# Attention and FFN on one core: a half's h and output tiles in pairs per PSUM bank, fewer scale operations, stores on SP's queue

## The chip, the core and the metric

The kernel runs on one core of a Trainium2 chip. Its engines are named as in the profile: PE (TensorE, matmuls; PEld its weight loads), DVE (VectorE), ACT (ScalarE), POOL (GpSimd) and SP (SyncE, which here only issues transfers). Each executes its own list of instructions in the order in which the program was built; semaphores tie the lists together. ACT and SP also issue DMAs, and such an issue stands in the engine's list like any other instruction. The metric is the device time of a run in microseconds (us), the median of several runs.

## The reference

```python
scores = scale * q @ k.T                                  # B=8, H=8, S=576, D=64
cum    = cumsum(maximum(s, 0))
scores = where(causal, -1e9, scores + minimum(-(cum_i - cum_j), 0))
attn   = softmax(scores) @ v
x      = attn.transpose(0, 2, 1, 3).reshape(4608, 512)
h      = x @ w_in                                         # 512 -> 2048
g      = where(h >= 1, h, where(h <= -1, 0, (h + 1)**2 / 4))
out    = g @ w_out                                        # 2048 -> 512
```

All inputs are fp32. The kernel computes each of the large products from f16 parts: every operand is scaled by powers of two and split into a high and a low half, and a product is three f16 matmuls (high x high, high x low, low x high).

## The kernel before

The work goes by batches of 576 tokens. A batch's tokens are the columns of its tiles, and they are cut into two halves (`HALF`): the first (`hf` 0) has 320 columns, the second (`hf` 1) 256.

**Attention** of a half is four jobs, one for each pair of heads. For a job, SP loads Q, K and V (`rq`, `rk` L337, `v` L254); ACT and DVE prepare them (L352 to L357); PE computes score tiles `s` (L412, L413); DVE masks them and takes the maximum `mn` (L418); ACT takes the exponential (L429, L451); POOL and DVE normalise and split (`rs` L445 and L446, `pb` L450 to L456); SP issues the DMA transposes `pt<-pb` (L457) and, once for both halves, `vt<-vb` (L383); PE multiplies them into `px` (L475); ACT and DVE write the half's f16 tile `x` (L486, L487). Score tiles and `px` share two PSUM banks.

**The FFN** of a half has 16 h tiles of 128 rows each. For tile `ft`, `ffn_h` lets PE put 12 matmuls into one of two PSUM banks `h` (L530). Then come, on 320 or 256 columns:

- ACT: `u` = Relu(us x h + ub) (L542);
- DVE: two passes, `h` = max(ws x h, u) (L545) and `u` = min(u, r) x h (L546);
- ACT: the f16 cast of `u`, g's high part (L556). `g_split` issues it behind the next tile's Relu, so that ACT's list runs Relu, cast of the tile before, Relu, cast;
- POOL: g's low part, `u` less the cast (L557).

`ffn_y` then lets PE put 12 matmuls into the four banks `y0` to `y3`, one for each 128 rows of the output (L569). The y matmuls of a tile follow its h by `Y_LAG` = 2 tiles, and run on into the h tiles of the next half. After the sixteenth, four evictions `o` scale the banks into SBUF (ACT, L583; at the very end DVE takes two, L581), and each is stored with a DMA of its own (L584), on ACT's queue but for two at the end.

The scales us, ws, ub, r and the output's ys are small tiles of a batch, made by `batch_scales` (13 DVE operations, behind the reduction that makes `a_in` once, L615) and `batch_y` (two per batch, L304). The first batch's are made at the end of the start-up, ahead of the loads of w_out, whose staging tiles are first written from `a_in` (L184, in `load`).

Attention of the halves to come is woven into the FFN of the half at hand: `attention_ffn` walks over FFN steps (one h tile or one y tile each) and inserts a slot of an attention job at set places. A scheduler then fixes each engine's list, by priorities (`FFN_LEAD` for the FFN's passes and evictions, `X_LEAD` for `x`) and by the buffers' dependences; `tc.issue_after` pins an instruction behind another. A wait of one instruction thus holds up everything behind it in its engine's list, SP's transposes behind SP's loads among them.

w_in is decoded and split ahead of the first FFN tile, w_out beside the first halves.

Of the kernel before, what the change touches and what calls it, by code (L numbers as in the profile page):

```python
# [71 lines left out]
def attention_ffn(ctx: ExitStack, tc: tile.TileContext, qT, kT, vT, s, w_in, w_out, yT):  # L72
# [201 lines left out]

    def batch_scales(b):
        m = msc[b]
        h = hsc[b] = ap.tile([P, 4], F32, tag="hs", name=f"hs{b}")
        V.tensor_scalar(h, w1.bound, m, 2.0 ** -27, ALU.mult, ALU.mult)
# [4 lines left out]
        V.tensor_scalar(r, r, 1.0, None, ALU.max)
# [1 line left out]
        V.tensor_scalar(r, r, 2.0 ** 14, None, ALU.mult)
        V.tensor_scalar(i, i, 23, None, ALU.logical_shift_right)
        V.tensor_scalar(i, i, 127, None, ALU.add)
        V.tensor_scalar(i, i, 1, 23, ALU.logical_shift_right, ALU.logical_shift_left)
# [4 lines left out]
        V.tensor_scalar(w, u, 2.0, None, ALU.mult)
# [227 lines left out]
    ffn_q, g4 = [], [None]  # L521

    def ffn_h(b, hf, ft):
        h_off, N, _ = HALF[hf]
        x = X[b, hf]
        h = ps_h.tile([P, 512], F32, tag="h", name=f"h{b}_{hf}_{ft}")
        n = 0
        for kt in range(NKT):
            for wl, xl in ((0, 0), (0, 1), (1, 0)):
                T.matmul(  # L530
                    h[:, :N], WI[4 * kt + ft // 4][:, wl, ft % 4 * P:(ft % 4 + 1) * P], x[:, kt, xl],
                    start=(n == 0), stop=(n == 3 * NKT - 1),
                )
# [4 lines left out]
        g = g4[0][:, ft % 4]
        with tc.high_priority(offset=FFN_LEAD):

            u = gp.tile([P, N], F32, tag="u", bufs=4, name=f"u{b}_{hf}_{ft}")
            first = A.activation(u, h[:, :N], AF.Relu, bias=ubi[b], scale=usc[b][:, fg:fg + 1]).ins  # L542
# [2 lines left out]
            V.scalar_tensor_tensor(h[:, :N], h[:, :N], wsc[b][:, fg:fg + 1], u, ALU.mult, ALU.max)  # L545
            V.scalar_tensor_tensor(u, u, r, h[:, :N], ALU.min, ALU.mult)  # L546
# [5 lines left out]
    def g_split(first=None):  # L552
        while to_split:
            g, u = to_split.pop()
            with tc.issue_after(first) if first is not None else ExitStack():
                A.copy(g[:, 0], u)  # L556
            G.tensor_tensor(g[:, 1], u, g[:, 0], ALU.subtract)  # L557

    ys = {}

    def ffn_y(b, hf, ft, g, ms=tuple(range(NKT))):
# [4 lines left out]
        for m in ms:
            c0 = ft % 2 * 2 * P + m % 2 * P
            for n, (wl, gl) in enumerate(((0, 0), (1, 0), (0, 1))):
                T.matmul(  # L569
                    ys[b, hf, m][:, :N], WO[8 * (m // 2) + ft // 2][:, wl, c0:c0 + P], g[:, gl],  # L570
                    start=(ft == 0 and n == 0), stop=(ft == NFT - 1 and n == 2),
                )
        if ft == NFT - 1:
            last = (b, hf) == (B - 1, len(HALF) - 1)
            for m in ms:
                tag, bufs = ("u", 4) if last and m >= 2 else ("o", O_BUFS)
                o = gp.tile([P, N], F32, tag=tag, bufs=bufs, name=f"o{b}_{hf}_{m}")
                y = ys[b, hf, m][:, :N]
                with tc.high_priority(offset=FFN_LEAD):
                    if last and m % 2:  # L580
                        V.tensor_scalar(o, y, ysc[b][m // 2], None, ALU.mult)  # L581
                    else:
                        A.activation(o, y, AF.Copy, scale=ysc[b][m // 2])  # L583
                (nc.sync if last and m % 2 else nc.scalar).dma_start(  # L584
                    yT[m * P:(m + 1) * P, b * S + h_off:b * S + h_off + N], o
                )
# [28 lines left out]
    V.tensor_reduce(a_in, w1.bound, axis=AX, op=ALU.max)  # L615
# [77 lines left out]
```

## Time and profile before

| | us |
|---|---|
| runs | 1110.91, 1114.15, 1114.35 |
| median | 1114.15 |
| the profiled execution's own time | 1111.73 |
| its span in the profile | 1109.9 |
| mean granted TensorE clock | 0.963 |
| PE busy | 1010.8 |
| DVE, ACT, POOL busy | 846.3, 725.8, 679.0 |

The profile is of one execution, which took 1111.73 us by the same clock as the runs; 1.8 us of that lie outside the span. Times in the trace count from the start of the span. In the first 145 us the weights are loaded and split, and PE is busy for 82.5 of them; from 275 us on, one batch after another takes 122 to 124 us; after 1013 us no attention is left, and only the FFN of the last batch runs. A row of waits gives the engine and line that waited, who released it, the total in us, how often, and the longest. A row of a group gives line, engine, operation, out<-in, the shape and the count, then busy us and mean ns of one, then the idle time ahead of it and what ended it. A row of the timeline gives start and duration in us, and in brackets the wait ahead of it.

### The profile page before, as it was taken

The numbers are of one execution on the slowest core, as the hardware profiler recorded it, in microseconds if no ns is written. First come the engines' busy times: TensorE is split into PE (matmuls) and PEld (weight loads), VectorE is DVE, ScalarE is ACT, GpSimd is POOL, SyncE is SP. The second block draws the span as 40 slices with busy tenths as digits, with TensorE's granted clock in tenths as the row PEclk, the third lists the DMA queues.
The fourth block names the chain that finished last, engine by engine and source line by source line (L and its number), as shares of the span: only waits on it lengthen the run. The fifth ranks groups of instructions, "written<-read, shape, count | busy, mean of one in ns | idle before, by whom it ended". The sixth has DMA issues, their size and how long they took to land.

```text
span 1109.9 us, 25082 instructions
## 1 busy us (share of the span) xinstructions
PE 1010.8 (91%) x8495; PEld 774.9 (70%) x8496; DVE 846.3 (76%) x2325; ACT 725.8 (65%) x1703; POOL 679.0 (61%) x1173
## 2 busy tenths in 40 slices
PE   2456898799999999999999999899999999899998
PEld 1232466587768877777778877687778877787787
DVE  7887966688787877787778877787777887887533
ACT  4765985677567774867567765777576765777432
POOL 4782795775556764766467664666476665765522
PEclk9955999799999999999999999999999999999999
DMA  7876653786468663886468763877387763676300
GB/s 235 218 200 192 170 87 91 158 173 155 100 122 188 148 152 71 187 162 158 79 146 177 161 136 81 177 160 163 68 176 155 165 137 74 158 156 138 68 25 19
DMA packets 340775, 155.01 MB, mean 140 GB/s; under 512 B 290856, under 2 KB 322472, under 8 KB 340648
## 3 DMA queue, kind: packets, MB, share of 16 engines
q1 hardware_dynamic: 330944, 143.49, 59.6%
q10 hardware_dynamic: 9704, 9.93, 2.9%
q8 instruction: 67, 1.10, 0.4%
q14 instruction: 60, 0.49, 0.1%
HBM read 72.31 MB, written 9.73 MB: 74 GB/s over the span
## 4 chain that ended last, share of the span: by engine, by line
PE 61%; DVE 12%; POOL 8%; DMA 7%; issue 6%; ACT 5%; ACTq 0%; SPq 0%; DVEq 0%; POOLq 0%
PE y L569 25%; PE h L530 25%; PE px L475 4%; DMA pt<-pb 3%; PE s L412 3%; PE s L413 3%; DVE pb L456 2%; ACT u L542 2%; POOL pb L453 2%; POOL pb L450 2%; DVE p L418 1%; DVE Q L357 1%; DMA vt<-vb 1%; POOL vb L371 1%; DVE h L545 1%
## 5 line engine op out<-in xcount | busy, mean ns | idle before, releaser
L530 PE MATMUL h<-x,WI 128*128 128x256 f16 (+1 forms) x3072 | 463.9, 290 | 7.4 <-ACT x L486 3.4
L569 PE MATMUL y<-g,WO 128*128 128x256 f16 (+1 forms) x3072 | 457.8, 288 | 7.0 <-POOL g L557 5.3
L530 PEld LDWEIGHTS <-WI 128*128 128x128 f16 x3072 | 291.1, 99 | 97.0 <-issue 13.9
L569 PEld LDWEIGHTS <-WO 128*128 128x128 f16 x3072 | 288.1, 98 | 92.9 <-issue 13.8
L557 POOL TENSOR_TENSOR g<-u,g 128x320 f16<-128x320 f32 (+1 forms) x256 | 206.0, 805 | 152.1 <-ACT g L556 151.6
L429 ACT ACTIVATE p<-p,mn 64x64 f32<-64x64 f32 (+4 forms) x320 | 179.4, 561 | 142.7 <-DVE mn L418 122.2
L542 ACT ACTIVATE u<-h,ub,us 128x320 f32<-128x320 f32 (+1 forms) x256 | 149.1, 583 | 120.3 <-PE h L530 115.3
L545 DVE SCALAR_TENSOR_TENSOR h<-h,ws,u 128x320 f32<-128x320 f32 (+1 forms) x256 | 132.4, 517 | 110.6 <-ACT u L542 108.1
L450 POOL TENSOR_SCALAR pb<-p,rs 64x128 f16<-64x128 f32 (+4 forms) x160 | 95.3, 596 | 171.2 <-DVE rs L446 112.1
L453 POOL TENSOR_TENSOR pb<-p,pb 64x128 f16<-64x128 f32 (+4 forms) x160 | 173.9, 1087 | 9.5
L456 DVE SCALAR_TENSOR_TENSOR pb<-p,rs,pb 64x128 f16<-64x128 f32 (+4 forms) x160 | 134.6, 841 | 47.1 <-POOL pb L450 47.0
L418 DVE CUSTOM_DVE_ANT_0 p<-s,mask 64x64 f32<-64x64 f32 (+4 forms) x320 | 134.4, 420 | 31.3 <-PE s L413 23.0
L412 PE MATMUL s<-K,Q 128*64 128x64 f32 (+1 forms) x336 | 126.2, 377 | 16.0 <-DVE mn L418 10.9
L546 DVE SCALAR_TENSOR_TENSOR u<-u,r,h 128x320 f32<-128x320 f32 (+1 forms) x256 | 130.3, 509 | 6.8 <-DVE h L545 0.5
L451 ACT ACTIVATE p<-p,rs 64x64 f32<-64x64 f32 (+4 forms) x160 | 89.6, 560 | 51.3 <-DVE rs L446 49.4
L556 ACT CAST g<-u 128x320 f16<-128x320 f32 (+1 forms) x256 | 107.9, 421 | 10.3 <-DVE u L546 10.3
L413 PE MATMUL s<-K,Q 68*64 68x64 f32 (+1 forms) x336 | 102.8, 307 | 2.1 <-DMA K<-cumd 1.3
L452 POOL TENSOR_SCALAR pb<-p 64x128 f16<-64x128 f32 (+4 forms) x160 | 93.2, 583 | 11.9 <-ACT p L451 11.0
L475 PEld LDWEIGHTS <-vt 128*64 128x64 f16 x1536 | 73.4, 113 | 36.7 <-issue 30.2
L475 PE MATMUL px<-pt,vt 128*64 128x256 f16 (+3 forms) x1536 | 83.5, 259 | 13.3 <-DMA pt<-pb 8.7
L412 PEld LDWEIGHTS s<-K,Q 128*64 128x64 f32 (+1 forms) x336 | 61.5, 183 | 27.3 <-DVE mn L418 8.2
L413 PEld LDWEIGHTS s<-K,Q 68*64 68x64 f32 (+1 forms) x336 | 61.9, 184 | 5.8 <-issue 1.7
(105 smaller groups left out, 983.0 us busy)
## 6 DMA issues: line engine op xcount, KB each, us to landing
...
```

The costliest lines, as they stand in the source:

```text
L412: T.matmul(sc[:R, :c1 - c0], Q1[:, hd, qo:qo + R], K1[:, hd, c0:c1], start=True, stop=False)
L413: T.matmul(sc[:R, :c1 - c0], Q2[:KC, hd, qo:qo + R], K2[:KC, hd, c0:c1], start=False, stop=True)
L418: ttr[0] = V.tensor_tensor_reduce(out=Pt[:R, c0:c1], in0=sc[:R, :c1 - c0], in1=mask[:R, mo:mo + c1 - c0], scale=-0.125 if j < F32_JOBS els ...
L429: A.activation(Pt[:R, :W], Pt[:R, :W], AF.Exp, bias=m2[:R], scale=-1.0, accum_out=sums[n, i][:R, hd:hd + 1])
L453: G.tensor_tensor(los[1], pw, his[1], ALU.subtract)
L456: V.scalar_tensor_tensor(los[0], pv, rs[:R, :1], his[0], ALU.mult, ALU.subtract)
L475: T.matmul(px[hd * D:(hd + 1) * D, lo:N], VT[:, vl * NB + j, hd * D:(hd + 1) * D], PT[:, 4 * j + 2 * hd + pl, lo:], start=(m == 0), stop=( ...
L530: T.matmul(h[:, :N], WI[4 * kt + ft // 4][:, wl, ft % 4 * P:(ft % 4 + 1) * P], x[:, kt, xl], start=(n == 0), stop=(n == 3 * NKT - 1),)
L542: first = A.activation(u, h[:, :N], AF.Relu, bias=ubi[b], scale=usc[b][:, fg:fg + 1]).ins
L545: V.scalar_tensor_tensor(h[:, :N], h[:, :N], wsc[b][:, fg:fg + 1], u, ALU.mult, ALU.max)
L557: G.tensor_tensor(g[:, 1], u, g[:, 0], ALU.subtract)
L569: T.matmul(ys[b, hf, m][:, :N], WO[8 * (m // 2) + ft // 2][:, wl, c0:c0 + P], g[:, gl], start=(ft == 0 and n == 0), stop=(ft == NFT - 1 an ...
```

## The change

Four things, of which the first is the largest.

1. In the second half (256 columns), two h tiles share a PSUM bank of 512 columns. Relu, both DVE passes, the cast and the low part then run once for a pair, on 512 columns. The four output tiles lie in pairs in the banks `y0` and `y1`; there are two evictions of 512 columns, in buffers of the `u` ring, and two stores of 128x2x256. Only the first tile of a y bank opens its accumulation with the start flag, and `issue_after` keeps the other's first matmul behind it.
2. `Y_LAG` is (2, 4): in the second half y follows h by four tiles, and up to two y tiles are issued in a step.
3. Of a batch's 13 + 2 scale operations 6 + 1 are left; factors that don't depend on the batch (`wb1`, `wb2`, 4 x `a_in`) are made once, `wb1` ahead of the first batch's scales.
4. All stores but the very last half's first are issued on SP's queue.

The first half's tiles and passes keep their shapes, and PE's list has the same number of instructions, 16170, in another order.

```diff
-Y_LAG = 2
+Y_LAG = (2, 4)
...
+    def weight_scales():
+        V.tensor_reduce(a_in, w1.bound, axis=AX, op=ALU.max)
+        V.tensor_scalar(a_in, a_in, 4.0, None, ALU.mult)
+        for i in range(2):
+            V.tensor_scalar(wb1[:, i], w1.bound, 2.0 ** (i - 27), None, ALU.mult)
...
     def batch_scales(b):
         m = msc[b]
-        h = hsc[b] = ap.tile([P, 4], F32, tag="hs", name=f"hs{b}")
-        V.tensor_scalar(h, w1.bound, m, 2.0 ** -27, ALU.mult, ALU.mult)
-
         r = rsc[b] = ap.tile([P, 1], F32, tag="r", name=f"r{b}")
         i = r.bitcast(I32)
-        V.tensor_scalar(r, m, a_in, 4.0, ALU.mult, ALU.mult)
-        V.tensor_scalar(r, r, 1.0, None, ALU.max)
-        V.reciprocal(r, r)
...
-        u = usc[b] = ap.tile([P, 4], F32, tag="us", name=f"us{b}")
-        V.tensor_scalar(u, h, r, None, ALU.mult)
-        w = wsc[b] = ap.tile([P, 4], F32, tag="ws", name=f"ws{b}")
-        V.tensor_scalar(w, u, 2.0, None, ALU.mult)
+        V.tensor_scalar(r, m, a_in, 1.0, ALU.mult, ALU.max)
+        V.tensor_scalar(i, i, 24, None, ALU.logical_shift_right)
+        V.tensor_scalar(i, i, -(2 ** 23), 197 * 2 ** 23, ALU.mult, ALU.add)
+
+        h = ap.tile([P, 2, 4], F32, tag="hs", name=f"hs{b}")
+        V.tensor_scalar(h, wb1, m, r, ALU.mult, ALU.mult)
+        usc[b], wsc[b] = h[:, 0], h[:, 1]
         c = ubi[b] = ap.tile([P, 1], F32, tag="ub", name=f"ub{b}")
         V.tensor_scalar(c, r, 0.5, None, ALU.mult)
         g = gsc[b] = ap.tile([P, 1], F32, tag="gb", name=f"gb{b}")
         V.reciprocal(g, r)
-        V.tensor_scalar(g, g, g, 2.0 ** 14, ALU.mult, ALU.mult)
 
...
     def batch_y(b, groups=(0, 1)):
-        ysc.setdefault(b, {})
+        y = ap.tile([P, 2], F32, tag="ys", name=f"ys{b}") if b else ys0
+        c = slice(groups[0], groups[-1] + 1)
+        if b == 0:
+            V.tensor_scalar(wb2[:, c], w2.bound[:, c], 2.0 ** -14, None, ALU.mult)
+        V.tensor_scalar(y[:, c], wb2[:, c], gsc[b], gsc[b], ALU.mult, ALU.mult)
         for i in groups:
-            y = ysc[b][i] = ap.tile([P, 1], F32, tag=f"ys{i}", name=f"ys{b}_{i}")
-            V.tensor_scalar(y, gsc[b], w2.bound[:, i:i + 1], 2.0 ** -28, ALU.mult, ALU.mult)
+            ysc.setdefault(b, {})[i] = y[:, i:i + 1]
...
     def ffn_h(b, hf, ft):
         h_off, N, _ = HALF[hf]
         x = X[b, hf]
-        h = ps_h.tile([P, 512], F32, tag="h", name=f"h{b}_{hf}_{ft}")
+        c = ft % 2 if hf else 0
+        if c == 0:
+            h2[0] = ps_h.tile([P, 512], F32, tag="h", name=f"h{b}_{hf}_{ft}")
+        h = h2[0]
         n = 0
         for kt in range(NKT):
             for wl, xl in ((0, 0), (0, 1), (1, 0)):
                 T.matmul(
-                    h[:, :N], WI[4 * kt + ft // 4][:, wl, ft % 4 * P:(ft % 4 + 1) * P], x[:, kt, xl],
+                    h[:, c * N:(c + 1) * N], WI[4 * kt + ft // 4][:, wl, ft % 4 * P:(ft % 4 + 1) * P], x[:, kt, xl],
                     start=(n == 0), stop=(n == 3 * NKT - 1),
...
-        g = g4[0][:, ft % 4]
+        if hf == 0 or c:
+            ffn_g(b, hf, ft, c + 1)
+        return g4[0][:, ft % 4]
+
+    def ffn_g(b, hf, ft, n):
+        N, r, fg = HALF[hf][1], rsc[b], ft // 4
+        h = h2[0][:, :n * N]
+        g = g4[0][:, ft % 4 + 1 - n:ft % 4 + 1]
         with tc.high_priority(offset=FFN_LEAD):
-
-            u = gp.tile([P, N], F32, tag="u", bufs=4, name=f"u{b}_{hf}_{ft}")
-            first = A.activation(u, h[:, :N], AF.Relu, bias=ubi[b], scale=usc[b][:, fg:fg + 1]).ins
+            u = gp.tile([P, n * N], F32, tag="u", bufs=U_BUFS, name=f"u{b}_{hf}_{ft}")
+            first = A.activation(u, h, AF.Relu, bias=ubi[b], scale=usc[b][:, fg:fg + 1]).ins
 
             g_split(first)
-            V.scalar_tensor_tensor(h[:, :N], h[:, :N], wsc[b][:, fg:fg + 1], u, ALU.mult, ALU.max)
-            V.scalar_tensor_tensor(u, u, r, h[:, :N], ALU.min, ALU.mult)
-        to_split.append((g, u))
-        return g
+            V.scalar_tensor_tensor(h, h, wsc[b][:, fg:fg + 1], u, ALU.mult, ALU.max)
+            V.scalar_tensor_tensor(u, u, r, h, ALU.min, ALU.mult)
+        to_split.append((g, u.rearrange("p (f n) -> p f n", f=n)))
 
     to_split = []
...
             with tc.issue_after(first) if first is not None else ExitStack():
-                A.copy(g[:, 0], u)
-            G.tensor_tensor(g[:, 1], u, g[:, 0], ALU.subtract)
-
-    ys = {}
+                A.copy(g[:, :, 0], u)
+            G.tensor_tensor(g[:, :, 1], u, g[:, :, 0], ALU.subtract)
...
     def ffn_y(b, hf, ft, g, ms=tuple(range(NKT))):
         h_off, N, _ = HALF[hf]
+        w = 1 + hf
         if ft == 0:
             for m in ms:
-                ys[b, hf, m] = ps_y.tile([P, 512], F32, tag=f"y{m}", name=f"y{b}_{hf}_{m}")
+                if m % w == 0:
+                    ys[b, hf, m // w] = ps_y.tile([P, 512], F32, tag=f"y{m // w}", name=f"y{b}_{hf}_{m // w}")
         for m in ms:
             c0 = ft % 2 * 2 * P + m % 2 * P
             for n, (wl, gl) in enumerate(((0, 0), (1, 0), (0, 1))):
+                opens = ft == 0 and n == 0
+                with tc.issue_after(opened[0]) if opens and m % w else ExitStack():
+                    opened[0] = T.matmul(
+                        ys[b, hf, m // w][:, m % w * N:(m % w + 1) * N],
+                        WO[8 * (m // 2) + ft // 2][:, wl, c0:c0 + P], g[:, gl],
+                        start=(opens and m % w == 0), stop=(ft == NFT - 1 and n == 2 and m % w == w - 1),
+                    ).ins
         if ft == NFT - 1:
...
+            for i in sorted({m // w for m in ms}):
+                tag, bufs = ("u", U_BUFS) if hf else ("o", O_BUFS)
+                o = gp.tile([P, w, N], F32, tag=tag, bufs=bufs, name=f"o{b}_{hf}_{i}")
+                y = ys[b, hf, i][:, :w * N]
+                on_v = last and i
+                scale = ysc[b][i * w // 2]
                 with tc.high_priority(offset=FFN_LEAD):
...
                     else:
-                        A.activation(o, y, AF.Copy, scale=ysc[b][m // 2])
+                        A.activation(o.rearrange("p m n -> p (m n)"), y, AF.Copy, scale=scale)
+                (nc.scalar if last and not i else nc.sync).dma_start(
+                    yT[i * w * P:(i + 1) * w * P, b * S + h_off:b * S + h_off + N].rearrange("(m p) n -> p m n", p=P), o
                 )
...
             ffn_q.append((b, hf, ft, ffn_h(b, hf, ft)))
-        elif len(ffn_q) > Y_LAG:
-            ffn_y(*ffn_q.pop(0))
+        else:
+            n = len(ffn_q) - Y_LAG[hf]
+            for _ in range(min(n, 2)):
+                ffn_y(*ffn_q.pop(0))
...
-    V.tensor_reduce(a_in, w1.bound, axis=AX, op=ALU.max)
+    weight_scales()
     batch_scales(0)
```

Beside the names: `ffn_g` is the part of `ffn_h` that issued the passes; `w` in `ffn_y` is the number of output tiles in a bank. In the rows of the change's list the lines are shifted by it: Relu L555, DVE passes L558 and L559, cast L568, low part L569, y L585, eviction L602, store L603, h L538, `x` L491, exponential L434 and L456, scores L417 and L418, loads L342, transposes L462 and L388.

More of the change, by code (lines that the diff above doesn't have):

```diff
@@ L48 @@
 G_BUFS = 4
+U_BUFS = 4
 O_BUFS = 3
 WO_LAG = 2
-Y_LAG = 2
+Y_LAG = (2, 4)
 ACT_LOW = {'wi': range(0, 16, 2), 'wo': range(0, 16, 2)}
@@ L247, in attention_ffn @@
     a_in = cp.tile([P, 1], F32, name="a_in")
-    vraw, csc, rcs, exs, hsc, rsc, usc, wsc, ubi, gsc, ysc, msc = ({} for _ in range(12))
+    vraw, csc, rcs, exs, rsc, usc, wsc, ubi, gsc, ysc, msc = ({} for _ in range(11))
     def load_v(b):
@@ L273, in batch_scales_v @@
         V.tensor_scalar(e, csc[b], r, 2.0 ** -12, ALU.mult, ALU.mult)
+    wb1 = cp.tile([P, 2, 4], F32, name="wb1")
+    wb2 = cp.tile([P, 2], F32, name="wb2")
+    ys0 = cp.tile([P, 2], F32, name="ys0")
+    def weight_scales():
[3 more added lines that the diff above has]
+            V.tensor_scalar(wb1[:, i], w1.bound, 2.0 ** (i - 27), None, ALU.mult)
     def batch_scales(b):
         m = msc[b]
-        h = hsc[b] = ap.tile([P, 4], F32, tag="hs", name=f"hs{b}")
-        V.tensor_scalar(h, w1.bound, m, 2.0 ** -27, ALU.mult, ALU.mult)
         r = rsc[b] = ap.tile([P, 1], F32, tag="r", name=f"r{b}")
         i = r.bitcast(I32)
-        V.tensor_scalar(r, m, a_in, 4.0, ALU.mult, ALU.mult)
-        V.tensor_scalar(r, r, 1.0, None, ALU.max)
-        V.reciprocal(r, r)
[L285 to L288, printed above, removed]
-        u = usc[b] = ap.tile([P, 4], F32, tag="us", name=f"us{b}")
-        V.tensor_scalar(u, h, r, None, ALU.mult)
-        w = wsc[b] = ap.tile([P, 4], F32, tag="ws", name=f"ws{b}")
-        V.tensor_scalar(w, u, 2.0, None, ALU.mult)
+        V.tensor_scalar(r, m, a_in, 1.0, ALU.mult, ALU.max)
[4 more added lines that the diff above has]
+        usc[b], wsc[b] = h[:, 0], h[:, 1]
         c = ubi[b] = ap.tile([P, 1], F32, tag="ub", name=f"ub{b}")
@@ L518, in att_slot @@
             att_out(*jobs[j - 1])
-    ffn_q, g4 = [], [None]
+    ffn_q, g4, h2 = [], [None], [None]
     def ffn_h(b, hf, ft):
@@ L568, in ffn_y @@
             for n, (wl, gl) in enumerate(((0, 0), (1, 0), (0, 1))):
[L569 to L572, printed above, removed]
+                opens = ft == 0 and n == 0
[5 more added lines that the diff above has]
+                    ).ins
         if ft == NFT - 1:
             last = (b, hf) == (B - 1, len(HALF) - 1)
[L575 to L578, printed above, removed]
+            for i in sorted({m // w for m in ms}):
[4 more added lines that the diff above has]
+                scale = ysc[b][i * w // 2]
                 with tc.high_priority(offset=FFN_LEAD):
-                    if last and m % 2:
-                        V.tensor_scalar(o, y, ysc[b][m // 2], None, ALU.mult)
-                    else:
-                        A.activation(o, y, AF.Copy, scale=ysc[b][m // 2])
-                (nc.sync if last and m % 2 else nc.scalar).dma_start(
-                    yT[m * P:(m + 1) * P, b * S + h_off:b * S + h_off + N], o
+                    if on_v:
+                        V.tensor_scalar(o.rearrange("p m n -> p (m n)"), y, scale, None, ALU.mult)
+                    else:
+                        A.activation(o.rearrange("p m n -> p (m n)"), y, AF.Copy, scale=scale)
+                (nc.scalar if last and not i else nc.sync).dma_start(
+                    yT[i * w * P:(i + 1) * w * P, b * S + h_off:b * S + h_off + N].rearrange("(m p) n -> p m n", p=P), o
                 )
```

2 lines of the change are left out of this document (1 added, 1 removed).

## The prediction

> **What bounds the kernel now.** I read the page's busy line first, then the windows by stage, then PE's waits in the steady stage. The busy line, and the windows' busy time of PE, VectorE (DVE), ScalarE (ACT) and GpSimd (POOL) by stretch:
>
> ```profile
> span 1109.9 us, 25082 instructions
> PE 1010.8 (91%) x8495; PEld 774.9 (70%) x8496; DVE 846.3 (76%) x2325; ACT 725.8 (65%) x1703; POOL 679.0 (61%) x1173
> ...
> 145.00:275.00 130.00, 118.52 (x998) 91.22 (x996) 93.79 (x264) 88.83 (x210) 93.39 (x154) 0.95 0.64 135
> 275.00:1013.00 738.00, 716.77 (x6328) 564.86 (x6327) 586.51 (x1658) 502.21 (x1222) 458.49 (x835) 0.99 0.66 141
> ```
>
> The columns of a stretch are its length, the busy time of PE, its weight loads, VectorE, ScalarE and GpSimd with their instructions, and the granted clock. PE is busy for all but 11.5 us of the stretch from 145 to 275, in which w_out is still being prepared, and for all but 21.2 of the 738 us of the steady stage, there at a granted clock of 0.99. The change leaves PE's instructions as they are in kind and number, so it can gain only where PE waits. Those waits, for 275 to 1013 (total us, times, longest), then the same for 145 to 275:
>
> ```profile
> PE s L412 <- DVE mn L418: 7.0, 9, 1.9
> PE y L569 <- POOL g L557: 4.9, 6, 1.3
> PE s L412 <- DVE Q L357: 4.2, 5, 1.5
> PE y L569 <- ACT g L556: 1.4, 6, 0.4
> ...
> PE px L475 <- DMA pt<-pb: 4.5, 1, 4.5
> PE s L412 <- DVE mn L418: 3.9, 3, 1.8
> PE h L530 <- DVE u L546: 1.0, 2, 0.8
> ```
>
> The waits for the FFN's own passes (g and u) are 7.3 us, those for VectorE in the scores (mn and Q) 15.1. Nearly everything that this change can win lies in these 22.4 us, 2% of the span; the rest of PE's time is streaming, which it leaves alone.
>
> **The wide passes.** A group by shape gives each pass of 256 and 320 columns (busy us, mean ns):
>
> ```profile
> L569 PE MATMUL y<-g,WO 128*128 128x256 f16 x1536 | 206.8, 274 | 5.5 <-POOL g L557 5.3
> L557 POOL TENSOR_TENSOR g<-u,g 128x320 f16<-128x320 f32 x128 | 113.0, 883 | 114.3 <-ACT g L556 114.2
> L557 POOL TENSOR_TENSOR g<-u,g 128x256 f16<-128x256 f32 x128 | 92.9, 726 | 37.8 <-ACT g L556 37.4
> L542 ACT ACTIVATE u<-h,ub,us 128x320 f32<-128x320 f32 x128 | 77.9, 609 | 75.3 <-PE h L530 73.0 <-POOL vb L371 1.8 <-POOL p L402 0.2
> L542 ACT ACTIVATE u<-h,ub,us 128x256 f32<-128x256 f32 x128 | 71.2, 556 | 45.0 <-PE h L530 42.3 <-PE s L413 2.3
> ...
> L545 DVE SCALAR_TENSOR_TENSOR h<-h,ws,u 128x320 f32<-128x320 f32 x128 | 70.8, 554 | 77.5 <-ACT u L542 75.2
> L546 DVE SCALAR_TENSOR_TENSOR u<-u,r,h 128x320 f32<-128x320 f32 x128 | 69.3, 542 | 2.7
> L545 DVE SCALAR_TENSOR_TENSOR h<-h,ws,u 128x256 f32<-128x256 f32 x128 | 61.5, 481 | 33.0 <-ACT u L542 32.9
> L546 DVE SCALAR_TENSOR_TENSOR u<-u,r,h 128x256 f32<-128x256 f32 x128 | 60.9, 476 | 4.1 <-DVE h L545 0.5
> L556 ACT CAST g<-u 128x320 f16<-128x320 f32 x128 | 57.4, 448 | 8.6 <-DVE u L546 8.6
> L556 ACT CAST g<-u 128x256 f16<-128x256 f32 x128 | 50.5, 395 | 1.7 <-DVE u L546 1.7
> ```
>
> Carrying each pair of shapes on to 512 columns in a straight line, an estimate, I get u 0.77 us, L545 0.77, L546 0.74, cast 0.61, low part 1.35. Two passes of 256 cost 1.11, 0.96, 0.95, 0.79 and 1.45. So 64 pairs take 33 us from ScalarE, 26 from VectorE and 6 from GpSimd. All of that lies beside PE and is worth nothing by itself.
>
> The chain of a pair becomes longer: 0.77+0.77+0.74+0.61+1.35 = 4.24 us where one tile's was 0.56+0.48+0.48+0.40+0.73 = 2.64. Against it stands the lag: y follows h by two tiles before (24 matmuls) and four after (48). In a row of the tail, quoted below, 36 such matmuls take 4.09 us, 0.114 each. So the cover goes from 2.7 to 5.5 us and the margin over the chain from nothing to 1.2, before what attention's passes add to both. The waits y<-POOL g all stand on the 256-column form, 5.3 us in its row; I take them as gone: **-5.3** (0 where queueing on GpSimd eats the margin). The same row names no wait for ACT's cast, so y<-ACT g (1.4) lies on the first half's form; it stays, since that half keeps its lag of two.
>
> **VectorE's relief.** The scales' operations run from 145 to 653 ns, and a longest wait of the scores looks like this:
>
> ```profile
> L293 DVE TENSOR_SCALAR ws<-us 128x4 f32<-128x4 f32 x8 | 5.2, 653 | 0.0
> ...
> L283 DVE TENSOR_SCALAR r<-r 128x1 f32<-128x1 f32 x8 | 1.2, 145 | 0.0
> ...
> DVE pb L456 <- POOL pb L450: 2.8, 3, 1.9
> ...
> 575.33 0.33 PE L412 MATMUL s<-K,Q 128*128 128x192 f32 x1 [1.95 <-DVE mn L418]
> ```
>
> VectorE loses 26 us of passes and, by eight operations fewer in each of eight batches at 0.15 to 0.65, some 10 to 15 of scales: 4 to 5% of its 846. But the longest wait for mn (1.95) stands right behind a wait of VectorE for GpSimd's pb of 1.9, in the stretch from 565 to 592, and the change doesn't touch that pb. A 0.77 us pass also holds up a score that comes behind it longer than one of 0.48. I take a third of the mn waits (10.9), a quarter of Q's (4.2) and half of h<-DVE u (1.0): **-3.6, -1.0, -0.5**. From nothing, or 2 us lost, to all 16.1 gained is open.
>
> **The change of batch.** On ScalarE's queue, where batch 3 ends and 4 begins, before (`u4_0_0` is the next batch's first Relu, `g3_1_12` the last g of the old one):
>
> ```order
> L542 ACTIVATE u3_1_15_9128<-h3_1_15_9115,ub3_6693,us3_6689 128x256
> L556 CAST g3_1_12_8969<-u3_1_14_9084 128x256
> L429 ACTIVATE p17_3_0_8997,sm17_3_8996<-p17_3_0_8997,mn17_3_0_0_9002 128x448
> L429 ACTIVATE p17_3_1_9026,sm17_3_8996<-p17_3_1_9026,mn17_3_1_0_9031 128x448
> L451 ACTIVATE p17_3_1_9026<-p17_3_1_9026,rs17_3_9036 128x448
> L542 ACTIVATE u4_0_0_9215<-h4_0_0_9201,ub4_8716,us4_8712 128x320
> L556 CAST g3_1_12_8969<-u3_1_15_9128 128x256
> ```
>
> Here only the last tile's cast stands behind the next batch's Relu; the one before it is cast three rows earlier. The same place after:
>
> ```order
> L491 ACTIVATE x4_0_7949<-px19_0_8609,ex4_7358 128x320
> L434 ACTIVATE p16_4_1_8570,sm16_4_8529<-p16_4_1_8570,mn16_4_1_288_8598 128x576
> L361 ACTIVATE Q2_89<-rq17_1_8511 64x2x256
> L456 ACTIVATE p16_4_1_8570<-p16_4_1_8570,rs16_4_8602 128x576
> L555 ACTIVATE u4_0_0_8894<-h4_0_0_8880,ub4_8426,hs4_8424 128x320
> L568 CAST g3_1_12_8662<-u3_1_15_8807 128x2x256
> L434 ACTIVATE p17_3_0_8684,sm17_3_8683<-p17_3_0_8684,mn17_3_0_0_8689 128x448
> ```
>
> The cast that stands behind `u4_0_0` now holds both of the last tiles, where only the last one was held before. On PE, this is what then lies between the end of `h4_0_0` and the first y of the old half's last two tiles:
>
> ```order
> L538 MATMUL h4_0_0_8880<-x4_0_7949,WI12_126 128x320
> L538 LDWEIGHTS WI12_126
> L538 MATMUL h4_0_1_8935<-x4_0_7949,WI12_126 128x320
> L538 LDWEIGHTS WI12_126
> L538 MATMUL h4_0_1_8935<-x4_0_7949,WI12_126 128x320
> L417 MATMUL s17_4_0_0_8750<-K1_1822,Q1_1821 128x288
> L418 MATMUL s17_4_0_0_8750<-K2_90,Q2_89 128x288
> L585 LDWEIGHTS WO7_137
> L585 MATMUL y3_1_0_8209<-g3_1_12_8662,WO7_137 128x256
> ```
>
> Two h matmuls and two score passes are all that PE has while it waits for that cast. Their times before, with the Relu's:
>
> ```profile
> 628.27 0.40 PE L412 MATMUL s<-K,Q 128*128 128x288 f32 x1
> 628.65 0.72 PE L530 MATMUL h<-x,WI 128*128 128x320 f16 x4
> ...
> 630.13 0.60 ACT L542 ACTIVATE u<-h,ub,us 128x320 f32<-128x320 f32 x1
> 630.63 0.39 ACT L556 CAST g<-u 128x256 f16<-128x256 f32 x1
> ```
>
> Cover: 0.38 for the scores (from 628.27 to the h matmuls at 628.65) and two h matmuls of 0.14 (four begin 0.55 before the next row of PE), 0.65 us. Chain: 0.60 + 0.61 + some 0.15 of handover. So PE waits 0.7 us at each of seven changes: **+4.9**, between 0 and the 2.56 of Relu, cast and low part uncovered (+17.9).
>
> **Start and tail.** Ahead of the copies that release the w_out loads stand, on VectorE:
>
> ```profile
> 72.32 0.15 DVE L615 TENSOR_REDUCE a_in<-bound_wi 128x1 f32<-128x4 f32 x1
> 72.50 0.29 DVE L278 TENSOR_SCALAR hs<-bound_wi,mb 128x4 f32<-128x4 f32 x1
> 73.18 0.25 DVE L184 COPY wor<-a_in 128x1 int32<-128x1 int32 x3
> ...
> 1101.91 4.09 PE L569 MATMUL y<-g,WO 128*128 128x256 f16 x36
> 1105.72 0.84 ACT L583 ACTIVATE o<-y,ys 128x256 f32<-128x256 f32 x2 [1.43 <-PE y L569]
> ```
>
> One more four-wide and one more one-wide operation there cost 0.29 + 0.15: **+0.4** (0 to 1). At the end the last pair's chain (4.24 and 0.5 of handover) outlasts 36 matmuls and two y passes by some 0.4 us, and one wide eviction for two gives 0.2 back: **+0.2** (-0.3 to 1).
>
> **The stores on SP.** ScalarE's queue issued 62 of them, and SP stood waiting long ahead of its transposes:
>
> ```profile
> L584 ACTq DMA_DIRECT2D out_dram<-o x62: 338/368/1758, 177.6 to 1106.7; - x62
> ...
> L583 ACT ACTIVATE o<-y,ys x4: 521/523/526, 580.9 to 585.8; 128x320 f32<-128x320 f32 x4
> ...
> SPq L457 <- DVE pb L456: 93.9, 62, 4.0
> ...
> 585.78 2.56 SPq L337 DMA_DIRECT2D rq<-in_q_dram  x2
> ...
> 590.96 1.43 SPq L457 DMA_TRANSPOSE pt<-pb  x1
> ```
>
> SP, first to second half of batch 3, before:
>
> ```order
> L457 DMA_TRANSPOSE pt17_0_8024<-pb17_0_8025 128x4x64
> L337 DMA rk19_0_8282<-in_k_dram 64x2x320 x2
> L457 DMA_TRANSPOSE pt17_0_8024<-pb17_1_8092 128x8x128
> L337 DMA rq19_0_8281<-in_q_dram 64x2x320 x2
> L383 DMA_TRANSPOSE vt18_8342<-vb18_8219 128x10x128
> L457 DMA_TRANSPOSE pt17_0_8024<-pb17_2_8150 128x12x128
> ```
>
> Nothing but loads and transposes stands there. The same place after:
>
> ```order
> L603 DMA out_0_dram<-o3_0_2_8179 128x320
> L462 DMA_TRANSPOSE pt17_0_7796<-pb17_1_7864 128x8x128
> L342 DMA rq19_0_8034<-in_q_dram 64x2x320 x2
> L603 DMA out_0_dram<-o3_0_3_8182 128x320
> L462 DMA_TRANSPOSE pt17_0_7796<-pb17_2_7922 128x12x128
> ```
>
> Each half-batch now puts two or four stores, each waiting for its eviction, ahead of transposes that PE's px needs. In the trace the last of these evictions ends at 586.3, and the transpose behind it begins at 590.96: over 4 us of slack, with 0.37 us per issue to fit in. Nothing charged: 0. ScalarE's 62 x 0.37 = 23 us was not what PE waited for.
>
> **The sum.** -5.3 -3.6 -1.0 -0.5 +4.9 +0.4 +0.2 = -4.9, from the profiled execution's 1111.73 (span 1109.9): 1106.8. That execution lies 2.4 below the median of the runs, inside their spread of 1110.91 to 1114.35; from the median the same step gives 1109.2. A measurement here tells 0.3% (3.3 us) from no change.
>
> **Rivals.** (1) *Larger gain*: the waits for g, mn, Q and u go, all but ACT g's (5.3 + 10.9 + 4.2 + 1.0 = 21.4), and no new one comes: 1090. For it: VectorE is the busiest engine behind PE and loses the most. Against it: mn's wait on GpSimd. Chance 0.14.
>
> (2) *No change*: VectorE's waits stay, since a longer pass holds the scores as long as the saved ones freed, and the batch change takes the 5.3 back: 1109 to 1114. Chance 0.18.
>
> (3) *Slower, by the wide pass at the batch change*: Relu, cast and low part all uncovered, 7 x 2.56 = 17.9, against 10.4 gained and 0.6 lost: 1119.8. It decides where the wait passes 1.4 us per change, since 7 x 1.4 equals the gains less the rest; for it, the cast's place in the order; against it, the 0.65 us of cover, and that only each y tile's third product needs the low part. Chance 0.13. The Trainium skill, Perfetto Trace Analysis, section Optimizing Scalar/DVE Operations, says that where these engines aren't saturated but cause bubbles elsewhere, breaking instructions up may finish work sooner. By that rule merging passes is the wrong way here, and the 65% and 76% in the busy line with waits behind g and mn agree with its condition; it would give this rival's time.
>
> (4) *Slower, by SP*: a store whose eviction is late stands ahead of a transpose and px waits. It decides when an eviction is over 4 us later than in this trace; 2 us lost at each of 14 half ends: 1111.7 + 28 = 1140. For it, the one 4.5 us px wait; against it, the slack. Chance 0.09.
>
> On (4), the same page of the Trainium skill, section DMA Optimizations, would have inputs and outputs issued by different engines; the change ends that, and no run shown here has them on one.
>
> **Chances and range.** The forecast, 1101 to 1112 by its open terms, has 0.46. Faster: 0.14, 0.37 of the forecast and 0.03 of (2) make 0.54; same: the rest of both, 0.24; slower: 0.13 + 0.09 = 0.22. The range goes down to 1092, into (1), and up to 1120, taking in (3); outside are (4) and half of (1).
>
> **What would show it.** Right: y<-POOL g gone from PE's waits; seven waits of y for ACT's cast near 0.7 us; wide passes at 0.74 to 0.77 us, the low part at 1.35; px<-pt unchanged. Wrong: px waits behind SP, waits for mn that grow, or waits of y over 1.4 us at the batch changes.

## The result, and the profile after

The change makes the kernel slower: 1141.72 us against 1114.25, a ratio of 1.025 with a 95% interval of 1.0218 to 1.0283. That is 27.5 us, where 4.9 fewer were forecast. The profiled execution took 1139.12 us. Its page, the same stretch by windows (275 to 1037) and PE's waits there, with one row of the kernel before (275 to 1013) as the last:

```profile
span 1137.3 us, 24576 instructions
PE 1012.3 (89%) x8496; PEld 773.7 (68%) x8496; DVE 843.3 (74%) x2138; ACT 703.1 (62%) x1560; POOL 675.6 (59%) x1109
...
275.00:1037.00 762.00, 718.45 (x6360) 564.98 (x6359) 591.45 (x1519) 487.05 (x1116) 462.16 (x793) 1.00 0.66 137
...
PE px L480 <- DMA pt<-pb: 9.4, 12, 1.6
PE y L585 <- POOL g L569: 8.8, 14, 1.4
PE s L417 <- DVE mn L423: 5.7, 11, 1.0
PE s L417 <- DVE Q L362: 4.4, 4, 1.2
PE y L585 <- ACT g L568: 4.0, 6, 0.7
PE h L538 <- DVE u L559: 3.3, 6, 0.6
PE px L480 <- issue: 3.3, 3, 1.5
PE s L417 <- ACT Q L361: 2.9, 2, 1.5
...
PE px L475 <- DMA pt<-pb: 0.8, 2, 0.6
```

Attention does not end where these stretches do, as I had written of 1013: its last px starts at 1048.7 us before and at 1075.1 after, 36 and 38 us later. The two stretches can be compared all the same. PE does the same work (1012.3 us busy, 1010.8 before). It waits 43.6 us in the steady stage (762.00 - 718.45) where it waited 21.2, so 22 of the 27 us are lost there. No single wait holds the loss: the transposes pt give 8.6 us more, "issue" 3.3, GpSimd's g 3.9, the cast of g 2.6, u 3.3, Q 3.1 (2.9 of it from ACT). Of the larger ones only mn fell, by 1.3; a wait of 1.3 for K from cumd is gone.

The passes themselves came out as worked out, the low part even shorter (forecast 0.77, 0.77, 0.74, 0.61, 1.35 us):

```profile
L569 POOL TENSOR_TENSOR g<-u,g 128x512 f16<-128x512 f32 x64 | 74.5, 1164 | 30.4 <-ACT g L568 30.3
...
L555 ACT ACTIVATE u<-h,ub,hs 128x512 f32<-128x512 f32 x64 | 49.1, 767 | 36.2 <-PE h L538 36.2
L558 DVE SCALAR_TENSOR_TENSOR h<-h,hs,u 128x512 f32<-128x512 f32 x64 | 48.0, 751 | 31.4 <-ACT u L555 31.3
L559 DVE SCALAR_TENSOR_TENSOR u<-u,r,h 128x512 f32<-128x512 f32 x64 | 47.4, 740 | 1.1
L568 ACT CAST g<-u 128x512 f16<-128x512 f32 x64 | 38.8, 607 | 4.9 <-DVE u L559 4.9
```

And this is the change of batch 3 to 4, in order of time on ACT and PE:

```profile
641.89 0.40 PE L417 MATMUL s<-K,Q 128*128 128x288 f32 x1
641.91 0.62 ACT L555 ACTIVATE u<-h,ub,hs 128x320 f32<-128x320 f32 x1 [1.69 <-PE h L538]
...
642.42 0.61 ACT L568 CAST g<-u 128x512 f16<-128x512 f32 x1
...
643.08 0.60 PE L585 MATMUL y<-g,WO 128*128 128x256 f16 x4 [0.66 <-ACT g L568]
```

The Relu of the new batch stands ahead, the wide cast of the old one follows, and PE waits 0.66 us. The same wait stands at all six changes of this stretch (4.0 us); the seventh change, before 275, has none.

### The profile page after: what moved, and what is told of

Read it like the earlier page. It is cut to its first block, busy times and chain, and to the rows that moved or that the text cites. A ratio compares the mean times of both kernels' runs of the same rounds, so it can differ in the third digit from the quotient of the medians.

```text
span 1137.3 us, 24576 instructions
## 1 busy us (share of the span) xinstructions
PE 1012.3 (89%) x8496; PEld 773.7 (68%) x8496; DVE 843.3 (74%) x2138; ACT 703.1 (62%) x1560; POOL 675.6 (59%) x1109
## 4 chain that ended last, share of the span: by engine, by line
PE 45%; DVE 18%; DMA 14%; POOL 9%; issue 8%; ACT 4%; ACTq 0%; SPq 0%; POOLq 0%; DVEq 0%
PE y L585 19%; PE h L538 17%; DMA pt<-pb 8%; PE px L480 4%; DVE pb L461 4%; DVE p L423 3%; POOL pb L455 3%; DMA vt<-vb 3%; PE s L417 2%; DVE u L559 2%; DMA wor<-in_moe_w_out_dram 2%; PE s L418 2%; POOL g L569 2%; DVE h L558 2%; POOL pb L458 1%
## 5 line engine op out<-in xcount | busy, mean ns | idle before, releaser
L538 PE MATMUL h<-x,WI 128*128 128x256 f16 (+1 forms) x3072 | 461.6, 290 | 9.3 <-DVE u L559 5.1
L585 PE MATMUL y<-g,WO 128*128 128x256 f16 (+1 forms) x3072 | 447.1, 287 | 14.5 <-POOL g L569 9.4
L585 PEld LDWEIGHTS <-WO 128*128 128x128 f16 x3072 | 286.8, 98 | 103.0 <-issue 23.3
L538 PEld LDWEIGHTS <-WI 128*128 128x128 f16 x3072 | 287.6, 99 | 98.0 <-issue 16.8
L434 ACT ACTIVATE p<-p,mn 64x64 f32<-64x64 f32 (+4 forms) x320 | 178.6, 558 | 157.2 <-DVE mn L423 125.0
L569 POOL TENSOR_TENSOR g<-u,g 128x320 f16<-128x320 f32 (+1 forms) x192 | 186.4, 971 | 135.7 <-ACT g L568 135.5
L461 DVE SCALAR_TENSOR_TENSOR pb<-p,rs,pb 64x128 f16<-64x128 f32 (+4 forms) x160 | 148.6, 929 | 73.4 <-POOL pb L455 73.3
L555 ACT ACTIVATE u<-h,ub,hs 128x320 f32<-128x320 f32 (+1 forms) x192 | 126.9, 661 | 117.6 <-PE h L538 116.1
L558 DVE SCALAR_TENSOR_TENSOR h<-h,hs,u 128x320 f32<-128x320 f32 (+1 forms) x192 | 118.8, 619 | 88.8 <-ACT u L555 86.2
L458 POOL TENSOR_TENSOR pb<-p,pb 64x128 f16<-64x128 f32 (+4 forms) x160 | 166.7, 1042 | 8.9
L417 PE MATMUL s<-K,Q 128*64 128x64 f32 (+1 forms) x336 | 127.7, 380 | 18.4 <-DVE mn L423 9.6
L456 ACT ACTIVATE p<-p,rs 64x64 f32<-64x64 f32 (+4 forms) x160 | 89.5, 559 | 61.8 <-DVE rs L451 60.0
L559 DVE SCALAR_TENSOR_TENSOR u<-u,r,h 128x320 f32<-128x320 f32 (+1 forms) x192 | 116.7, 608 | 4.7
L457 POOL TENSOR_SCALAR pb<-p 64x128 f16<-64x128 f32 (+4 forms) x160 | 108.6, 679 | 4.6 <-ACT p L456 3.3
L568 ACT CAST g<-u 128x320 f16<-128x320 f32 (+1 forms) x192 | 96.2, 501 | 17.5 <-DVE u L559 17.5
L418 PE MATMUL s<-K,Q 68*64 68x64 f32 (+1 forms) x336 | 103.4, 308 | 1.1 <-POOL K L365 0.6
L417 PEld LDWEIGHTS s<-K,Q 128*64 128x64 f32 (+1 forms) x336 | 61.5, 183 | 33.7 <-DVE mn L423 10.6
L365 DVE TENSOR_TENSOR K<-rk,K 64x1152 fp32r<-64x1152 f32 (+1 forms) x52 | 63.5, 1221 | 4.3 <-ACT K L360 3.1
```

The lines of the kernel that those rows point to most:

```text
L417: T.matmul(sc[:R, :c1 - c0], Q1[:, hd, qo:qo + R], K1[:, hd, c0:c1], start=True, stop=False)
L434: A.activation(Pt[:R, :W], Pt[:R, :W], AF.Exp, bias=m2[:R], scale=-1.0, accum_out=sums[n, i][:R, hd:hd + 1])
L458: G.tensor_tensor(los[1], pw, his[1], ALU.subtract)
L461: V.scalar_tensor_tensor(los[0], pv, rs[:R, :1], his[0], ALU.mult, ALU.subtract)
L538: T.matmul(h[:, c * N:(c + 1) * N], WI[4 * kt + ft // 4][:, wl, ft % 4 * P:(ft % 4 + 1) * P], x[:, kt, xl], start=(n == 0), stop=(n == 3 * ...
L558: V.scalar_tensor_tensor(h, h, wsc[b][:, fg:fg + 1], u, ALU.mult, ALU.max)
```

## The experiments

In all tables and sums below a time is the median of a kernel's runs, and a ratio is to the kernel before in the same comparison. "Moved" counts the rows that stand at another place when the lists of two kernels are laid side by side (of 8450 rows of PE, its matmuls but for two, and 2327 of DVE in the kernel before).

### The stores on SP

e1, the change with its stores back on ACT's queue:

```diff
-                (nc.scalar if last and not i else nc.sync).dma_start(
+                (nc.sync if last and i else nc.scalar).dma_start(
```

> The changed kernel with one thing undone: the stores are issued on ACT's queue again, as in the kernel before. Queue theory (stores ahead of transposes on SP's list cost most of the 27 us): PE's waits px<-pt fall from 17 us to the 9 of before, POOL's waits for the pt and vt transposes with them, and the time falls to 1112 to 1122. Pair theory (the longer passes cost most): px<-pt falls a little, y<-POOL g stays at 9 and the time stays at 1132 to 1142.

Measured 1133.27, ratio 1.0171 (1.0134 to 1.0209); 20 matmuls of PE move and nothing on DVE. So the stores cost 0.8%, 8 to 9 us, and 1.7% is left. The time lies at the lower end of the pair theory's range, not in the queue theory's. With the stores back on ACT's queue PE's waits in the steady stage (275 to 1032) are these:

```profile
PE s L417 <- DVE Q L362: 6.7, 6, 1.5
PE y L585 <- POOL g L569: 6.6, 8, 3.3
...
PE px L480 <- DMA pt<-pb: 6.0, 8, 1.4
```

Of the change's 9.4 us of px<-pt, 3.4 go with the stores, and 2.2 of its 8.8 us of y<-POOL g. The rest stays, and so do the waits for Q: 7.0 here with ACT's part, 7.3 in the change.

e2, the kernel before with its stores on SP:

```diff
-                (nc.sync if last and m % 2 else nc.scalar).dma_start(
+                (nc.scalar if last and not m % 2 else nc.sync).dma_start(
```

> The kernel before with one thing changed: its 62 stores (those of the last half as in the change, two on ACT) are issued on SP's queue. Queue theory: 1130 to 1142, px<-pt in PE's waits at 15 us or more; it has more stores than the change (four per second half, not two), so it should lose at least as much from this. Pair theory: 1110 to 1118, px<-pt at 9.

Measured 1122.43, ratio 1.0076 (1.0052 to 1.01), with 62 matmuls and 24 rows of DVE moved: again 8 to 9 us, between the ranges of the two theories, and not by waits of px for transposes, as I expected (1.8 us of them in the steady stage). PE's longest waits in the steady stage of e2, and SP's for its stores:

```profile
PE s L412 <- DVE Q L357: 8.8, 7, 1.6
PE y L569 <- POOL g L557: 7.3, 8, 1.4
PE s L412 <- DVE mn L418: 6.3, 9, 1.3
...
SPq L584 <- ACT o L583: 13.5, 11, 2.3
```

SP stands 13.5 us before stores whose evictions aren't done, with loads and transposes behind them. GpSimd's waits for the vt transpose, ahead of its vb and so of g, grow; before, then e2:

```profile
POOL vb L370 <- DMA vt<-vb: 30.2, 20, 3.3
...
POOL vb L370 <- DMA vt<-vb: 37.2, 20, 3.7
```

PE's waits for g go from 4.9 to 7.3 us. Its waits for Q double (4.2, now 8.8), but no engine waits for Q's loads `rq` in the steady stage of either kernel, so why Q is late isn't shown. At one place of batch 3, SP before:

```profile
584.41 1.25 SPq L457 DMA_TRANSPOSE pt<-pb  x1
585.78 2.56 SPq L337 DMA_DIRECT2D rq<-in_q_dram  x2
589.52 1.34 SPq L383 DMA_TRANSPOSE vt<-vb  x1
```

and in e2, where the kernel runs some 8 us later by then:

```profile
592.59 2.21 SPq L457 DMA_TRANSPOSE pt<-pb  x1
594.89 1.25 SPq L337 DMA_DIRECT2D rq<-in_q_dram  x2
596.19 1.56 SPq L584 DMA_DIRECT2D out_dram<-o  x3
597.85 1.88 SPq L383 DMA_TRANSPOSE vt<-vb  x1
```

Three stores take 1.56 us of SP's list ahead of the vt transpose. At this place they cost it little, since the loads before them take less: it starts 5.26 us behind the pt transpose, 5.11 before.

### The scales and the lag alone

e3 takes only the new scales (`weight_scales`, `batch_scales`, `batch_y` of the change) into the kernel before; e4 only the lag:

```diff
-Y_LAG = 2
+Y_LAG = (2, 4)
...
-        elif len(ffn_q) > Y_LAG:
-            ffn_y(*ffn_q.pop(0))
+        else:
+            n = len(ffn_q) - Y_LAG[hf]
+            for _ in range(min(n, 2)):
+                ffn_y(*ffn_q.pop(0))
```

> The kernel before with the new scales alone (7 operations a batch for 15, three more once at the start). Both theories: no more than 3 us either way, 1110 to 1117. If it is slower by more, the start (copies ahead of w_out's loads later by 0.4 us or more) or a shifted order is a third cause.

> The kernel before with the lag of (2, 4) and up to two y tiles in a step, h tiles unpaired. My forecast had this as the source of its gain: y<-POOL g falls from 5.3 us to under 1, and the time is 1106 to 1112. Pair theory: the same, since the loss is in the wide passes. If y<-POOL g stays or the time rises, the new order on PE is a cause by itself.

Measured: e3 1130.94, 1.0156 (1.0123 to 1.0189); e4 1124.29, 1.0097 (1.0069 to 1.0124). Both theories missed. And the lag of four did not do what the forecast had it do: with the 256-column passes as they were, y<-POOL g in e4's steady stage is

```profile
PE y L569 <- POOL g L557: 4.8, 4, 1.6
```

where it was 4.9. In e3, fewer and smaller operations on VectorE are unlikely to cost 17 us by their own time. What these edits do besides is to make the scheduler lay the lists out anew (177 matmuls and 155 rows of DVE, the ones taken out among them, for e3; 1905 and 432 for e4). So a third theory, of the order: the kernel before stands in an order that few others match.

### Edits that do nothing

Three edits to the kernel before, to test that. e5 and e6 multiply ub by 1, once and four times a batch; e7 changes a priority.

```diff
         V.tensor_scalar(c, r, 0.5, None, ALU.mult)
+        V.tensor_scalar(c, c, 1.0, None, ALU.mult)
...
-X_LEAD = 6000
+X_LEAD = 5000
```

> The kernel before with one idle operation more per batch: ub is multiplied by 1 once again on DVE (0.15 us, eight times, off PE's path). The scheduler lays the lists out anew for it: 1583 of PE's 8450 matmuls and 478 of DVE's rows stand at another place. Order theory (the kernel before has a favourable order, and any edit that moves the lists loses 10 us or more, whatever it does): 1122 to 1132. Work theory (each edit costs what its own operations cost): 1112 to 1116.

> The kernel before with four such idle operations per batch (0.6 us of DVE, eight times). Here only 165 matmuls of PE and 68 rows of DVE move, as few as with the new scales alone. Order theory: 1118 to 1132, near the 1131 of the new scales. Work theory: 1113 to 1118.

> The kernel before with X_LEAD 5000 for 6000: not one operation is added, removed or changed, only priorities; 655 matmuls of PE and 172 rows of DVE move. Order theory: 1118 to 1130. Work theory: the work is the same, 1111 to 1117.

Measured: e5 1135.23, 1.0177 (1.0162 to 1.0192); e6 1126.85, 1.0105 (1.0088 to 1.0122); e7 1124.08, 1.0069 (1.0051 to 1.0087). An idle operation of 0.15 us per batch makes the kernel 20 us longer, a little more than the order theory's range. The first row here is PE's largest wait of the steady stage in e5, the second that in e6; the third is from e6's page:

```profile
PE y L570 <- POOL g L558: 14.4, 18, 2.1
...
PE s L416 <- DVE Q L361: 11.5, 11, 2.8
...
PE 1018.6 (91%) x8495; PEld 777.5 (69%) x8496; DVE 851.1 (76%) x2357; ACT 728.3 (65%) x1703; POOL 677.0 (60%) x1173
```

The two waits were 4.9 and 4.2 us before. Another order, another wait. But waits are not all of it: PE is busy for 1019.6, 1018.6 and 1017.4 us in the profiled executions of e5, e6 and e7, and for 1010.8 before, with the same matmuls. That is 7 to 9 of the 23, 15 and 13 us by which their spans are longer; the last section comes back to it.

e12 is the control, a priority in the kernel before that moves almost nothing:

```diff
-FFN_LEAD = 6000
+FFN_LEAD = 5000
```

> The kernel before with FFN_LEAD 5000 for 6000: no operation is changed, and almost nothing moves (29 matmuls of PE, 2 rows of DVE, 1 of ACT, 2 of POOL, none of SP). If the loss grows with what moves: 1112 to 1117. If the kernel before is a needle that any move breaks: 1120 or more.

Measured 1114.5, 1.001 (0.9994 to 1.0026): with the order kept, the time is kept.

### The pairs, and the cast at the batch change

e8 is the change with the old scales and the stores on ACT's queue, which leaves pairs and lag.

> The changed kernel with the old 15 scale operations and the stores on ACT's queue: what is left of the change is the pairs and the lag of (2, 4). Work theory (new scales cost 17 by themselves, the stores 8): 1113 to 1120. Order theory (pairs or not, every other order costs 10 to 20): 1123 to 1136, and ACT g at each batch change at 0.66 us as in the change.

Measured 1123.62, 1.0067 (1.0044 to 1.0089): no more than any of the three edits that do nothing. e10 adds four idle operations to e8, e11 has a lag of three:

```diff
-Y_LAG = (2, 4)
+Y_LAG = (2, 3)
```

> The kernel with pairs, old scales and stores on ACT's queue, with four idle operations of DVE more per batch; 310 matmuls of PE and 88 rows of DVE move. Order theory: pairs in another order scatter like the unpaired kernel in other orders (1124 to 1135): 1118 to 1136. Work theory: within 4 us of the 1123.6 without the idle operations.

> The kernel with pairs, old scales and stores on ACT's queue, with a lag of (2, 3): y follows h by three tiles in the second half. The margin of my forecast shrinks by one tile (12 matmuls, 1.4 us), so y<-POOL g should rise from 3.1 us in the steady stage to 6 or more if the lag is what hides the pair's chain; the time 1118 to 1136 by the order theory, 1126 to 1130 if only that wait counts.

Measured: e10 1132.76, 1.0183 (1.0152 to 1.0213); e11 1135.02, 1.0196 (1.0161 to 1.0232). Both lie in the order theory's range. With the shorter lag y<-POOL g is, as expected, three times that of e8 (3.1):

```profile
PE y L581 <- POOL g L565: 9.9, 8, 2.7
```

e9 casts a batch's last pair at once, in e8:

```diff
         to_split.append((g, u.rearrange("p (f n) -> p f n", f=n)))
+        if hf and ft == NFT - 1:
+            with tc.high_priority(offset=FFN_LEAD):
+                g_split()
```

> The kernel of the run with pairs, old scales and stores on ACT's queue, with one thing more: a batch's last pair is cast at once, not behind the next batch's first Relu. My forecast's step for the batch change (a wait of 0.7 us at each of seven changes): y<-ACT g, 3.2 us in that run's steady stage, falls to under 0.6. The lists move again (1786 matmuls of PE), so the time can go either way: 1115 to 1135 by the order theory, 1118 to 1121 if only the wait counts.

Measured 1112.23, 0.9985 (0.9967 to 1.0004), the kernel before's time, and better than either theory had it. PE's waits there, for 275 to 1013, all of them:

```profile
PE s L414 <- DMA K<-cumd: 11.0, 6, 2.7
PE px L476 <- DMA pt<-pb: 1.8, 3, 1.4
PE s L413 <- DVE Q L358: 1.5, 5, 0.3
PE h L534 <- DVE u L555: 1.4, 3, 0.8
PE s L413 <- DVE x L488: 0.9, 5, 0.2
PE s L413 <- DVE mn L419: 0.2, 1, 0.2
```

Here the gain of the forecast can be seen: the waits for g are gone, mn and Q fell from 11.2 us to 1.7. And most of it is given back at one place, where K's part from cumd, issued on ACT's queue, lands late (one wait of 1.3 us for it before). e17 pins K's cast behind both cumd transfers in that kernel:

```diff
-        CUMQ.dma_start(K2[D + 2:D + 4, :, :W].bitcast(F32), cd[:, :, :W])
-        A.copy(K1[:, :, :W], rk)
+        kd = CUMQ.dma_start(K2[D + 2:D + 4, :, :W].bitcast(F32), cd[:, :, :W]).ins
+        with tc.issue_after(kd):
+            A.copy(K1[:, :, :W], rk)
```

> The early-cast kernel (pairs, old scales, stores on ACT), with K's f32 cast pinned behind both transfers from cumd, so that K's part is issued up to 0.8 us earlier; 1724 matmuls of PE move. If the order's other places stay as good: s<-K<-cumd falls from 11.0 us to under 7, and 1106 to 1111, ahead of both kernels. Order theory: the wait falls and the time is 1112 to 1130 all the same.

Measured 1151.9, 1.0341 (1.027 to 1.0412), the slowest of all and above what either theory had. The wait for cumd is gone from s, and others have come, these two the largest:

```profile
PE s L414 <- DVE mn L420: 8.2, 9, 1.6
PE y L585 <- POOL g L569: 6.3, 9, 1.5
```

### Is it the early cast, or its order?

e13 is the change with the early cast; e14 is e9 with the stores on SP; e15 and e16 are e9 with one and four idle operations; e18 is e9 with the new scales.

> The changed kernel, all its parts, with a batch's last pair cast at once and not behind the next batch's first Relu. Early-cast theory (that wait is the pairs' cost, 4.0 us in the change, and what follows from it): y<-ACT g under 0.6 us and 1120 to 1134. Order theory: 1125 to 1145, at random, y<-ACT g gone all the same.

> The early-cast kernel (pairs, old scales; 1112 us with stores on ACT's queue), stores on SP's queue as in the change; 367 matmuls of PE and 69 rows of DVE move. Queue theory: plus 8 to 10 us, 1119 to 1124, and more px<-pt in PE's waits. If the queue cost only arises in bad orders: 1110 to 1116.

> The early-cast kernel (pairs, old scales, stores on ACT) with one idle operation of DVE more per batch; 1361 matmuls of PE move. Early-cast theory: 1109 to 1117. Order theory (its 1112 was a lucky order): 1120 to 1136.

> The early-cast kernel (pairs, old scales, stores on ACT) with four idle operations of DVE more per batch; 326 matmuls of PE move. Early-cast theory: 1110 to 1118. Order theory: 1118 to 1136.

> The early-cast kernel (pairs, stores on ACT) with the new scales: the change itself but for the stores, with the early cast. 427 matmuls of PE move. If the new scales cost nothing by themselves: as the idle-operation variants of this kernel, 1112 to 1128. If they cost (17 us in the kernel before): 1128 to 1140.

| | us | ratio | 95% interval |
|---|---|---|---|
| e13, change with early cast | 1133.14 | 1.0178 | 1.0135 to 1.0222 |
| e14, e9 with stores on SP | 1121.40 | 1.0074 | 1.0052 to 1.0095 |
| e15, e9 with one idle operation | 1126.77 | 1.0128 | 1.0090 to 1.0165 |
| e16, e9 with four idle operations | 1122.90 | 1.0086 | 1.0054 to 1.0118 |
| e18, e9 with new scales | 1118.76 | 1.0036 | 1.0005 to 1.0067 |

Both theories hold a part. e9's 1112 was a favourable order (e15 and e16 lose 1% from edits that do nothing). But kernels that differ only in the early cast and in what the scheduler makes of it can be paired, and the early one is ahead each time: e9 to e8 -0.8%, e18 to e1 -1.3%, e16 to e10 -1.0%, e13 to the change -0.7% (here alone the two intervals touch). The same can be done for the stores on SP: +0.8% (e2 to before), +0.8% (the change to e1), +0.9% (e14 to e9), +1.4% (e13 to e18).

## Why the prediction was wrong

**The account.** The kernels in between give it step by step, in ratios: pairs and lag 0.7% (e8), new scales 1.0% more (e1), stores on SP 0.8% more (the change). Of these only the last can be pinned to the edit, since e1 and e2 leave PE's and DVE's lists nearly as they are (e1 the more so: 20 and 0 rows, while e6 lost 1.0% with 165 and 68). The 1.0% "of the scales" is what idle operations cost as well (e10 over e8: 1.2%), and the 0.7% lies within what edits that do nothing make of the unpaired kernel (0.7 to 1.8%).

**The step that failed** is the sum itself: "-5.3 -3.6 -1.0 -0.5 +4.9 +0.4 +0.2", counted on a kernel that stays as it is elsewhere. The change lays out all lists anew, and e5, e6 and e7 show that in the unpaired kernel this alone costs 8 to 20 us. The sum had no term for it, and no rival either. The one term that the runs pin down is a zero: the stores on SP cost 0.8%, 8 to 9 us. How much of the other 1.7% is order and how much the other edits, the runs don't separate. The clue was in the prediction's own rows: 15.1 us of waits for VectorE spread over 17 places, none of them with a slack that I had looked at.

**The wide passes** were sized rightly, each to 0.02 us but the low part (1.16 for 1.35).

**y<-POOL g, -5.3.** Wrong for the change: 8.8 us, not 0. The lag matters, since three tiles for four go with a wait of 9.9 us for 3.1 (e11, whose order differs too). But it does not remove the wait: with a lag of four it is 4.8 us in e4, 6.6 in e1, 6.1 in e10, and gone only in e9 and nearly so in e14 (1.1). What I had left out is what stands ahead of g in GpSimd's list. In the change 12 of the 14 waits stand behind an instruction of GpSimd that waited for one of SP's transposes, like this one:

```profile
481.68 0.48 POOL L455 TENSOR_SCALAR pb<-p,rs 128x256 f16<-128x256 f32 x1 [2.86 <-DMA pt<-pb]
482.12 1.16 POOL L569 TENSOR_TENSOR g<-u,g 128x512 f16<-128x512 f32 x1
```

**VectorE's relief, -3.6 and -1.0.** The relief itself did not come: I had counted 36 to 41 us off VectorE's 846, and its busy time is 843.3. The wide passes do take 27 us less; other passes take longer, such as this one (before, then after):

```profile
L456 DVE SCALAR_TENSOR_TENSOR pb<-p,rs,pb 128x256 f16<-128x256 f32 x32 | 20.7, 647 | 27.5 <-POOL pb L450 27.5
...
L461 DVE SCALAR_TENSOR_TENSOR pb<-p,rs,pb 128x256 f16<-128x256 f32 x32 | 29.1, 910 | 38.8 <-POOL pb L455 38.7
```

Why is not shown; it is 902 ns in e1, 927 in e8 and 681 in e9, so the stores and the scales aren't the cause. mn fell by 1.3 us in the steady stage, where a third of 7.0 would be 2.3; the waits for Q rose from 4.2 to 7.3, and stay at 7.0 with the stores back on ACT's queue (e1); h's waits for u rose by 3.3 us.

**The batch change, +4.9.** The wait was met, 0.66 us at each of six changes for 0.7 at seven; the 1.4 us on the first half's form, which I had left standing, is gone. Its price was not met: four pairs of kernels put the late cast at 0.7 to 1.3%, 8 to 15 us. Whether the rest comes from what the late y holds up behind it, the runs don't tell: each pair has its own order besides.

**The stores on SP, 0.** Wrong: 8 to 9 us in two comparisons with the lists kept. "Over 4 us of slack" was read at one place and for the one transpose. It held for px in e2 (1.8 us of waits), but not in the change, where 3.4 us of px<-pt go with the stores. And SP's list is one queue: GpSimd's waits for its transposes, vt and pt together, are longer with the stores on SP in all three pairs for which I add them up (41.8 us in e2 for 33.3 before, 63.2 in the change for 55.6 in e1, there by pt alone, 41.2 in e14 for 24.1 in e9). Rival (4) named the place and was priced at 28 us; it is a third of the loss, not all of it. That its time (1140) was the nearest is luck: px waits, its mechanism, hold 3.4 us of it.

**The two rules that the prediction quoted.** The Trainium skill, Perfetto Trace Analysis, section DMA Optimizations, says that it may make sense to issue inputs and outputs from different engines: e1 and e2 agree, by 0.8%. The advice of the Trainium skill on the same page (section Optimizing Scalar/DVE Operations) to break instructions up where these engines aren't saturated but cause bubbles elsewhere isn't borne out by these runs and isn't refuted: pairs gave 0.9985 to 1.0196 with stores on ACT (1.0341 where K's cast was pinned too), single tiles in other orders 1.0069 to 1.0177.

**What stays open.** What is good in the order of the kernel before was not found: each worse order loses at other places, and some also in PE's busy time. Whether the wide passes would gain in an order chosen for them with the same care stays open; e9 only equals the kernel before.
